# Program order through the output projection, and GpSimd kept to small instructions

## The chip, the cores and the metric

The kernel runs on one core of one Trainium2 chip. The time is device microseconds of one execution; three runs of the kernel before are shown with their median. TensorE (PE) multiplies, VectorE (DVE), ScalarE (ACT) and GpSimd (POOL) work on tiles, and SyncE (SP) issues most transfers. Each engine takes its instructions in the order of its own queue.

## The reference

One pre-norm transformer block: sliding-window attention, and a gated MLP that mixes over the sequence. S = 2048 tokens, D = 640, 32 heads of 20 columns, a window of 256 tokens, two gate halves of Fh = 864 columns.

```python
h  = x + A(layernorm(x))
h2 = h + B(layernorm(h))

def A(x):                                   # wqkv (D, 3D), wo (D, D)
    q, k, v = split_heads(x @ wqkv)         # 32 heads, 20 columns each
    p = softmax(where(window, q @ k.T * 20 ** -0.5, -1e9))
    return merge_heads(p @ v) @ wo

def B(x):                                   # w_in (D, 2 Fh), w_sp (S, S), w_out (Fh, D)
    z = gelu(x @ w_in)
    z1, z2 = z[..., :Fh], layernorm(z[..., Fh:])
    return (z1 * (w_sp @ z2 + b_sp[:, None])) @ w_out
```

## The kernel before

Products that need float32 accuracy are made from two parts: `hi`, the operand rounded for TensorE, and `lo`, the rest. `hi*hi`, `hi*lo` and `lo*hi` are added up in PSUM. So each operand costs a copy (the `hi`, mostly on ACT) and a subtraction (the `lo`, on DVE or POOL).

**Attention.** The scores are computed by steps `s`, one for a group of four heads and one block of 128 keys; step `s` makes the scores of item `s` and the product with V (`pv_item`) of item `s - 2`. The product for 256 tokens is copied out of PSUM into `ot` (L398 on ACT, L400 on DVE) and stored to the scratch `o_d` in DRAM. A 21st column of V gives the sums of the softmax. `inverse_sums` loads them from `o_d`, takes the reciprocal on DVE (L342) and stores it to `r_d`; it is a generator, advanced once per step, for 512 tokens at a time. Another generator, `proj_early`, uses the last sixteen steps to load and split wo (L180, L181) and to load, scale and split the first tiles of the attention's output.

**wo.** The loop at the end of `block_kernel` runs over 16 tiles of 128 tokens. `load_o` brings two tiles of `o_d` (five transfers of 128 KB) and the matching reciprocals; `norm_o` (L146) multiplies them; `split_o` makes `hi` and `lo` (L152 to L155); `proj_o` (L89) does 30 matmuls into one of two accumulators `acc`; L1165 adds x, which gives h. h is stored from ACT's queue (L1166), and `layernorm` (L73 to L79) makes the normed tile `hn`: statistics on DVE, two one-column steps on POOL, the scaling on DVE. `turn_h` transposes it with five PE instructions and stores it to `hn_d`. Into the same loop `win1_prep` weaves the preparation of the first half of w_in (`right_blocks`, L644), and `run(i - NT)` the first operands of the next stage.

**z and the gate.** A list `steps` of PE products follows, and `later` holds what is to be done around each (`at(n, f)`: `f` at step `n`). Eight `z_pair`s make the first half of z. Then come four `z2_pair`s (60 matmuls each, L886; gelu at L890; statistics at L908 to L913; scaling at L918; `right_blocks` makes the seven right operands of a seven-product block multiplication), eight `first_gate`s, four more `z2_pair`s and eight `second_gate`s, with the products of w_sp at L992. During the first second gate the rows of w_out are loaded one by one into a small buffer and split (`put_wout`, L122 and L123). In the z pairs and the gates the matmuls are long and the other engines prepare their operands a few steps ahead.

**Who sets the order.** In a `manual_schedule` context (`ms`) PE, DVE, ACT and SP take their instructions in the order of the program. The context ends at `ms.close()`, just ahead of the wo loop; from there on a planner orders each engine's queue by modelled times. POOL is not in the context's list.

Of the kernel before, what the change touches and what calls it, by code (L numbers as in the profile page):

```python
# [34 lines left out]
def block_kernel(ctx, tc, x, wqk, wv, wo, w_in, wsp, bsp, w_out, out):  # L35
# [13 lines left out]
    o_d = dram.tile([H, 32, S], F32, name="o_d")  # L49
# [31 lines left out]

    def gemm(ps, n, lhs, rhs, ks):

        lh, ll = lhs
        rh, rl = rhs
        for k in range(ks):
            for a, b in ((lh, rh), (lh, rl), (ll, rh)):
                for j in range(2):
                    nc.tensor.matmul(ps[:, j, :n], a(k), b(k, j),  # L89
                                     start=(k == 0 and a is lh and b is rh),  # L90
                                     stop=(k == ks - 1 and a is ll))
# [5 lines left out]
    def open_early(pl):  # L97
        mem["t1"] = pl.tile([P, 2 * KF * D], F32R, name="t1")
        mem["m1"] = pl.tile([P, 6 * D + 4 * P], F32, name="m1")
        mem["xh"] = [pl.tile([P, D], F32, name=f"xh{i}") for i in range(2)]  # L100
        mem["ho"] = [pl.tile([P, D], F32, name=f"ho{i}") for i in range(3)]
# [27 lines left out]
    def load_o(j):  # L129
# [3 lines left out]
        for k in range(KD):  # L133
            nc.sync.dma_start(ot[:, k], o_d[:, 4 * k:4 * k + 4, t])
# [3 lines left out]
        def load_rs():  # L138
            base = r_d[:, t]
            nc.sync.dma_start(rs, bass.AP(tensor=base.tensor, offset=base.offset, ap=[[S, H], [0, 4], [1, 2 * P]]))  # L140
# [3 lines left out]
    def norm_o(i, eng):  # L144
        ot, rs = ots[i]
        eng.tensor_tensor(out=ot, in0=ot, in1=rs[:, None, :].to_broadcast([P, KD, P]), op=OP.mult)  # L146

    def split_o(i, eng):
        ot, _ = ots[i]
        osp = mem["osp2"] if i % 3 == 2 else t1((2 * KD + i % 3 * 2) * D, 2, KD, P)  # L150
        if eng is nc.vector:
            eng.tensor_copy(out=osp[:, 0], in_=ot)  # L152
        else:
            nc.scalar.activation(osp[:, 0], ot, AF.Copy)
        eng.tensor_tensor(out=osp[:, 1], in0=ot, in1=osp[:, 0].bitcast(F32), op=OP.subtract)  # L155
        ots[i] = osp

# [7 lines left out]
    def proj_early():  # L165
# [10 lines left out]
        for _ in range(4):  # L176
            yield
        for k in range(KD):
# [3 lines left out]
            if k in (1, 3):  # L182
                yield
        yield
        rs = load_o(0)
        yield
        yield
        rs()
        yield
        yield  # L190
        load_o(1)()
        yield
        for i in range(2):
            norm_o(i, nc.vector)
            split_o(i, nc.vector)
            yield


    with ExitStack() as ab:
# [132 lines left out]
        def inverse_sums(c):  # L332
            t = tmp3.tile([P, P], F32, tag="inv", bufs=2, name=f"inv{c}")

            def rows(d, step):
                return bass.AP(tensor=d.tensor, offset=d.offset, ap=[[step, H], [P, 4], [1, P]])

            yield
            nc.sync.dma_start(t, rows(o_d[:, DH, c * 512:(c + 1) * 512], 32 * S))
# [3 lines left out]
            nc.sync.dma_start(rows(r_d[:, c * 512:(c + 1) * 512], S), t)  # L343
# [27 lines left out]
        def pv_item(u):  # L371
# [20 lines left out]
            if kb % 2:  # L392
# [4 lines left out]
                if u >= NU - 5 or j == 0 and u < NU - LEAD:  # L397
# [3 lines left out]
                nc.sync.dma_start(o_d[4 * g:4 * g + 4, :, e:e + 256].rearrange("h d t -> (h d) t"), ot)  # L401
            if kb % 4 == 3:
                if g == 7:
                    inverse.append(inverse_sums(c))
# [176 lines left out]
        for s in range(NU + 2):  # L581
# [5 lines left out]
            for hh in range(4):  # L587
# [9 lines left out]
                if hh == 2 + s - NU and s >= NU:  # L597
                    if s == NU:
                        psB.close()
                        psW = pool(psB, "psW", space=PSUM)  # L600
                    pre_ps.append(proj_o(s - NU, psW.tile([P, 2, 512], F32, tag="wo", bufs=3, name=f"wo_ps{s - NU}")))
                if s >= 2:
# [3 lines left out]
                    if hh == 3:  # L606
                        next(pv, None)
            if u1 == NU:
# [12 lines left out]
        for f in inverse:  # L621
            for _ in f:
                pass


    ms.close()
# [78 lines left out]
    def win1_prep(raw):  # L705
        seven, last = win1
        src = w_in[:, :FH].rearrange("k (h c) -> k h c", h=2)
        for k in range(2):
# [5 lines left out]
            for f in right_blocks(lambda: [s[k] for s in seven], *(raw[:, b, h] for b in range(2) for h in range(2)),  # L714
                                  eng=nc.gpsimd):
# [9 lines left out]
    def win2_prep(raw):  # L725
        for k in range(KD):
# [5 lines left out]
            minus(win2[0][:, 1, k], raw, win2[0][:, 0, k].bitcast(F32), nc.gpsimd)  # L732
# [33 lines left out]
    def turn_h(i):  # L766
        ht = mem["ho"][i % 3]
        if i < NT - 2:
# [99 lines left out]
    def z2_pair(q, i, j, k):  # L868
# [6 lines left out]
        def prep(t, first, eng):  # L875
# [3 lines left out]
            else:  # L879
                minus(a[t][:, 1], r3, a[t][:, 0].bitcast(F32), eng)  # L880
# [11 lines left out]
        for t, tile_t in ((0, i), (1, j)):  # L892
# [3 lines left out]
            at(m - (1 if soon else 3), lambda t=t: prep(t, True, None))  # L896
            at(m - (1 if soon else 2), lambda t=t: prep(t, False, nc.gpsimd if t else nc.vector))
# [6 lines left out]
        def stat(t, h):  # L904
# [4 lines left out]
            if h:  # L909
                nc.vector.bn_aggr(out=mv[:, 0:2], in_=st)  # L910
                nc.gpsimd.tensor_scalar(out=mv[:, 2:3], in0=mv[:, 1:2], scalar1=EPS, scalar2=None, op0=OP.add)
                nc.gpsimd.tensor_tensor(out=mv[:, 3:4], in0=mv[:, 2:3], in1=half, op=OP.pow)
                nc.gpsimd.tensor_scalar(out=mv[:, 2:3], in0=mv[:, 0:1], scalar1=mv[:, 3:4], scalar2=-1.0,  # L913
                                        op0=OP.mult, op1=OP.mult)

        def norm(t):
            mv = stats[t][1]
            nc.scalar.activation(z[t], z[t], AF.Identity, bias=mv[:, 2:3], scale=mv[:, 3:4])  # L918
# [11 lines left out]
    def gate_pair(p, c, post, extra):  # L930
# [13 lines left out]
        eng = nc.vector if p else nc.gpsimd  # L944

# [6 lines left out]
        def s13():  # L952
            plus(s1, a21, a22, eng=eng)
            minus(a21, a11, a21, eng)

        def s2():
            minus(a11, s1, a11, eng)
# [263 lines left out]
```

## Time and profile before

| | |
|---|---|
| runs, median of 3 | 1161.44 us (1158.47 to 1166.19) |
| the profiled execution | 1165.89 us |
| its span | 1163.7 us |
| mean granted PE clock | 0.984 |
| busy: PE, DVE, ACT, POOL | 1102.1, 736.8, 553.9, 404.8 us |
| moved by DMA | 165.35 MB |

A row of the timeline is: start, duration, engine, line, operation, output <- inputs, form, count, and in brackets how long the engine had been idle and which instruction or transfer ended that wait. A row of the groups has the busy time and the mean duration in ns, then the idle time before such instructions and what ended it. In the table by stage each engine has its busy time and its count of instructions; PEclk is the granted clock of PE as a share of full speed. Busy times of PE include waiting in its pipeline, so counts of matmuls say more than its busy time.

### The profile page before, as it was taken

What the parts mean: (1) busy time and instruction counts of PE and PEld (TensorE: products, weight loads), DVE (VectorE), ACT (ScalarE), POOL (GpSimd) and SP (SyncE); (2) the same over time, 40 slices, a digit from 0 to 9 for tenths busy, and PEclk for the clock granted to TensorE, in tenths of its full rate; (3) what the DMA queues carried; (4) which work ended last, traced back from release to release, by engine and by line L of the source; (5) the groups of instructions that cost most, each with busy time, mean ns of one, the idle gap of its engine ahead of it and who ended that gap; (6) DMA issues with size and microseconds to landing.
All of it is one profiled execution on the core that took longest, in us unless ns stands there. A gap on an engine that the chain in (4) does not pass through costs nothing.

```text
span 1163.7 us, 28646 instructions
## 1 busy us (share of the span) xinstructions
PE 1102.1 (95%) x11152; PEld 994.7 (85%) x11152; DVE 736.8 (63%) x1961; ACT 553.9 (48%) x1181; POOL 404.8 (35%) x530
## 2 busy tenths in 40 slices
PE   6999999999999999788999998999999799999998
PEld 6998886667877777588999997999999699999998
DVE  5541213788999986679858468655547874655542
ACT  4334433258998889534257566433336531222110
POOL 3124443456666667446421066000117420000000
PEclk9999999999999999889999999999999999999999
DMA  4222355545555543578736512232341454444332
GB/s 149 78 69 80 136 169 201 184 152 176 184 182 176 179 136 125 164 233 270 245 138 210 167 65 73 67 130 87 119 152 39 157 167 152 142 132 143 93 94 68
DMA packets 79800, 165.35 MB, mean 142 GB/s; under 512 B 10752, under 2 KB 43264, under 8 KB 75776
## 3 DMA queue, kind: packets, MB, share of 16 engines
q1 hardware_dynamic: 77360, 158.28, 42.0%
q10 hardware_dynamic: 2304, 5.24, 1.2%
q8 instruction: 87, 1.43, 0.5%
q14 instruction: 49, 0.40, 0.1%
HBM read 108.83 MB, written 54.66 MB: 140 GB/s over the span
## 4 chain that ended last, share of the span: by engine, by line
PE 62%; ACT 8%; issue 7%; POOL 7%; DVE 6%; DMA 6%; SPq 3%; ACTq 0%; POOLq 0%; DVEq 0%
PE g L992 21%; PE out_ps L1057 8%; ACT pt L363 5%; PE pv L386 4%; PE bank L300 3%; PE bank L361 3%; PE zx L835 2%; POOL sg L486 2%; PE zv L835 2%; PE zb L886 2%; PE zy L835 2%; PE zw L835 1%; PE wo_ps L89 1%; PE qk L467 1%; PE qk L468 1%
## 5 line engine op out<-in xcount | busy, mean ns | idle before, releaser
L363 ACT ACTIVATE pt<-bank 128x384 f32<-128x384 f32 (+2 forms) x512 | 202.5, 484 | 29.4 <-PE bank L361 22.3
L992 PE MATMUL g<-zl,aw 128*128 128x432 f32 x768 | 174.4, 363 | 8.8 <-ACT zl L650 8.3
L650 ACT ACTIVATE aw<-fx 128x512 fp32r<-128x512 f32 (+2 forms) x160 | 92.9, 595 | 187.3 <-PE g L992 122.3
L310 DVE CUSTOM_DVE_ANT_0 junk<-bank,strip 128x288 bf16<-128x288 f32 x392 | 156.2, 454 | 15.2 <-PE bank L300 13.8
L992 PEld LDWEIGHTS g<-zl,aw 128*128 128x128 f32 x768 | 145.4, 190 | 17.3 <-ACT zl L650 10.5
L992 PE MATMUL g<-ze,aw 128*128 128x432 f32 x576 | 136.2, 366 | 4.6 <-ACT aw L650 4.5
L386 PE MATMUL pv<-pt,v_sb 128*32 128x192 f32 (+3 forms) x1984 | 130.9, 326 | 10.1 <-DVE ot L400 5.0
L644 DVE TENSOR_TENSOR aw<-fx,aw 128x512 fp32r<-128x512 f32 (+2 forms) x152 | 111.9, 746 | 37.0 <-ACT aw L650 36.3
L992 PEld LDWEIGHTS g<-ze,aw 128*128 128x128 f32 x576 | 109.8, 192 | 10.3 <-ACT aw L650 5.2
L361 PE MATMUL bank<-slot 123*32 123x288 bf16 (+7 forms) x1536 | 110.0, 280 | 2.4 <-issue 1.1
L365 POOL TENSOR_SCALAR_AFFINE_SELECT pt<-pt 128x512 f32<-128x512 f32 x128 | 81.9, 640 | 70.6 <-ACT pt L363 69.3
L1057 PE MATMUL out_ps<-wout,y_sp 128*128 128x320 f32 (+1 forms) x630 | 96.2, 309 | 0.4 <-ACT y_sp L122 0.4
L886 PE MATMUL zb<-win,aw 128*128 128x432 f32 x480 | 95.3, 359 | 0.0
L1057 PEld LDWEIGHTS out_ps<-wout,y_sp 128*128 128x128 f32 (+1 forms) x630 | 94.1, 188 | 1.2 <-ACT y_sp L122 0.7
L886 PEld LDWEIGHTS zb<-win,aw 128*128 128x128 f32 x480 | 89.9, 187 | 4.7
L300 PE MATMUL bank<-slot 120*32 120x288 bf16 (+6 forms) x1280 | 92.2, 277 | 0.9 <-issue 0.8
L483 DVE TENSOR_TENSOR rest<-qk,sg 128x512 f32<-128x512 f32 x40 | 27.7, 692 | 89.5 <-ACT sg L481 89.5
L386 PEld LDWEIGHTS pv<-pt,v_sb 128*32 128x32 f32 x1984 | 61.9, 111 | 17.8 <-issue 14.3
L361 PEld LDWEIGHTS <-slot 123*32 123x32 bf16 x1728 | 60.3, 98 | 17.1 <-issue 8.3
L486 POOL TENSOR_TENSOR sg<-rest,sg 128x512 bf16<-128x512 f32 x40 | 46.5, 1164 | 75.1 <-ACT sg L485 73.2
L368 POOL TENSOR_SCALAR_AFFINE_SELECT pt<-pt 128x512 f32<-128x512 f32 x112 | 71.6, 639 | 0.0
L644 DVE TENSOR_TENSOR row<-g,row 128x432 f32<-128x432 f32 x80 | 48.2, 604 | 36.1 <-PE g L992 32.7
(192 smaller groups left out, 2221.1 us busy)
## 6 DMA issues: line engine op xcount, KB each, us to landing
slot<-qk_d SPq DMA_DIRECT2D x144, 160.0 KB
fx<-wsp_in SPq DMA_DIRECT2D x32, 512.0 KB
qk_d<-sg SPq DMA_DIRECT2D x40, 384.0 KB
fx<-hn_d SPq DMA_DIRECT2D x32, 320.0 KB
o_d<-ot SPq DMA_DIRECT2D x64, 128.0 KB
xb<-qk_d SPq DMA_DIRECT2D x48, 160.0 KB
z_d<-row SPq DMA_DIRECT2D x16, 432.0 KB
g_d<-row SPq DMA_DIRECT2D x16, 432.0 KB
```

What stands on the lines that cost most here:

```text
L300: nc.tensor.matmul(ps[32 * j:32 * j + 32, o:o + w], one(st, 120, 0, hh, q0, 32), k, start=True, stop=True, tile_position=(0, 32 * j))
L310: nc.vector.tensor_tensor_reduce(out=junk[:, :n], in0=ps[:, :n], in1=keep, scale=1.0, scalar=NEG, op0=OP.add, op1=OP.max, accum_out=m_cols ...
L361: nc.tensor.matmul(ps[32 * i:32 * i + 32, b + o:b + o + w], one(st, 123, 1, hh, k0, 32), q, start=True, stop=True, tile_position=(0, 32 * i))
L363: nc.scalar.activation(pt[:, hh, :n], ps[:, :n], AF.Exp, scale=SCALE)
L365: nc.gpsimd.affine_select(out=pt[:, :, :P], in_=pt[:, :, :P], pattern=[[0, 4], [1, P]], base=0, channel_multiplier=-1, compare_op=OP.is_ge ...
L386: nc.tensor.matmul(ps[32 * hh:32 * hh + 32, a - 512 * c:b - 512 * c], v_sb[:, kb, v0:v0 + 32], pt[:, hh, a - kb * P:b - kb * P], start=fir ...
L644: (eng or nc.vector).tensor_tensor(out=out, in0=a, in1=b, op=op)
L650: nc.scalar.activation(out, a, AF.Copy)
L835: nc.tensor.matmul(ps, a[x], b[:, y], start=start and m + x + y == 0, stop=stop and m == n - 1 and x == 1, skip_group_check=True)
L886: nc.tensor.matmul(b[0][:, :HF], a[t][:, x, kk], win2[0][:, y, kk, h * HF:(h + 1) * HF], start=kk + x + y == 0, stop=kk == KD - 1 and x == 1)
L992: nc.tensor.matmul(ps, w[m][:, x, k], zc[k][m][:, y], start=start and k + x + y == 0, stop=stop and k == 3 and x == 1, skip_group_check=True)
L1057: nc.tensor.matmul(ps[j][:, :HD], src[:w, a, k, :], e1["wout"][:w, b, k, j * HD:(j + 1) * HD], start=(k == 0 and a + b == 0), stop=(k == K ...
```

## The change

- `ms.close()` moves from ahead of the wo loop to the third step of the z stage: the wo loop runs in program order. The loop is written anew: an iteration `i` does the projection of tile `i`, the addition and statistics of tile `i - 1`, scaling and split of the attention's output of tile `i + 2`, the scaling of `hn` of `i - 1` and the transposes of `i - 2`.
- The scratch `o_d` is laid out by column, head and token, wo's rows are ordered to match, and `load_o` is one transfer instead of five.
- `inverse_sums` works on 256, 256, 512, 512 and 512 tokens, with one more step between the load and the reciprocal. `proj_early` starts one step sooner and takes one row block of wo per step.
- Within a step the PV product comes ahead of the early `proj_o`; two of the last `ot` copies move from ACT to DVE.
- Every wide subtraction or addition that POOL did from wo on is done by DVE. POOL keeps the one-column steps of the statistics, of which there are now three per tile in wo.
- The final scaling of `hn` moves from DVE to ACT (`scaled`), and the stores of h move from ACT's queue to SP's.
- In a `z2_pair` the scaling of the first row and the operands that follow from it come one step later in program order.

```diff
-    o_d = dram.tile([H, 32, S], F32, name="o_d")
+    o_d = dram.tile([32, H, S], F32, name="o_d")
...
+    def stats_of(mv, st):
+        nc.vector.bn_aggr(out=mv[:, 0:2], in_=st)
+        nc.gpsimd.tensor_scalar(out=mv[:, 2:3], in0=mv[:, 1:2], scalar1=EPS, scalar2=None, op0=OP.add)
+        nc.gpsimd.tensor_tensor(out=mv[:, 3:4], in0=mv[:, 2:3], in1=half, op=OP.pow)
+        nc.gpsimd.tensor_scalar(out=mv[:, 2:3], in0=mv[:, 0:1], scalar1=mv[:, 3:4], scalar2=-1.0,
+                                op0=OP.mult, op1=OP.mult)
+
+    def scaled(dst, src, mv):
+        nc.scalar.activation(dst, src, AF.Identity, bias=mv[:, 2:3], scale=mv[:, 3:4])
...
-        for k in range(KD):
-            nc.sync.dma_start(ot[:, k], o_d[:, 4 * k:4 * k + 4, t])
+        base = o_d[:, :, t]
+        nc.sync.dma_start(ot, bass.AP(tensor=base.tensor, offset=base.offset, ap=[[S, P], [P * S, KD], [1, 2 * P]]))
...
-        eng.tensor_tensor(out=osp[:, 1], in0=ot, in1=osp[:, 0].bitcast(F32), op=OP.subtract)
         ots[i] = osp
+        return lambda: nc.vector.tensor_tensor(out=osp[:, 1], in0=ot, in1=osp[:, 0].bitcast(F32), op=OP.subtract)
...
-        for _ in range(4):
+        for _ in range(3):
             yield
         for k in range(KD):
...
-            if k in (1, 3):
-                yield
-        yield
-        rs = load_o(0)
+            if k == 2:
+                rs0 = load_o(0)
+            yield
+        rs0()
+        rs1 = load_o(1)
         yield
         yield
-        rs()
-        yield
-        yield
-        load_o(1)()
+        rs1()
         yield
         for i in range(2):
-            norm_o(i, nc.vector)
-            split_o(i, nc.vector)
+            norm_o(i)
+            split_o(i, True)()
             yield
+        yield
+        norm_o(2)
...
-                if u >= NU - 5 or j == 0 and u < NU - LEAD:
+                if u >= NU - 2 or j == 0 and u < NU - LEAD:
...
-            if kb % 4 == 3:
-                if g == 7:
-                    inverse.append(inverse_sums(c))
+            if g == 7 and (kb % 4 == 3 or kb == 1):
+                n = 256 if kb < 4 else 512
+                inverse.append(inverse_sums((kb + 1) * P - n, n))
...
-        for f in inverse:
-            for _ in f:
-                pass
-    ms.close()
...
-            minus(win2[0][:, 1, k], raw, win2[0][:, 0, k].bitcast(F32), nc.gpsimd)
+            minus(win2[0][:, 1, k], raw, win2[0][:, 0, k].bitcast(F32))
...
-        f = right_blocks(lambda: zc[k], *blocks, nc.vector if k == 3 else nc.gpsimd)
+        f = right_blocks(lambda: zc[k], *blocks)
         at(n0 + 1, lambda: stat(0, 0))
-        at(n0 + 2, lambda: (stat(0, 1), norm(0), f[0](), f[1](), f[2]()))
-        at(n0 + 3, lambda: stat(1, 0))
+        at(n0 + 2, lambda: stat(0, 1))
+        at(n0 + 3, lambda: (stat(1, 0), norm(0), f[0](), f[1](), f[2]()))
...
-        eng = nc.vector if p else nc.gpsimd
...
-                split(e1["wout"][:, 0, k], e1["wout"][:, 1, k], e1["h"][k // 4], nc.gpsimd)
+                split(e1["wout"][:, 0, k], e1["wout"][:, 1, k], e1["h"][k // 4])
...
-    for i in range(NT):
-        if 1 < i + 1 < NT:
-            split_o(i + 1, nc.gpsimd)
-        if i % 2 == 0 and i + 4 < NT:
-            load_o(i // 2 + 2)()
+    stat_h = {}
+
+    def add_h(i):
+        h3 = hs[i].rearrange("p (a b) -> p a b", a=2)
+        nc.vector.tensor_tensor(out=h3, in0=pre_ps.pop(0)[:, :, :HD], in1=h3, op=OP.add)
+        nc.sync.dma_start(h_d[i], hs[i])
+
+    def bn_h(i):
+        st, mv = stat_h[i] = stat_tiles(f"c{i}")
+        for j in range(2):
+            nc.vector.bn_stats(out=st[:, j, :], in_=hs[i][:, j * HD:(j + 1) * HD])
+        stats_of(mv, st)
+
+    lows = {}
+    for i in range(1, NT + 1):
+        if i < NT:
+            for f in inverse:
+                next(f, None)
+                if i == 2:
+                    next(f, None)
+        if i == 1:
+            split_o(2)()
+        if 1 < i < NT:
+            pre_ps.append(proj_o(i, acc_tile(f"wo_ps{i}")))
+        if i > 1:
+            add_h(i - 1)
         if i + 2 < NT:
-            norm_o(i + 2, nc.vector)
-        for n in (2, 3, 4) if i == 0 else (i + 4,) if i + 4 < NT else ():
+            norm_o(i + 2)
+            lo = split_o(i + 2)
+        if i == 1:
+            add_h(0)
+        if i < NT:
+            run(i - NT)
+        bn_h(i - 1)
+        if i + 2 < NT:
+            lo()
+        if i == 1:
+            load_o(2)()
+        if i % 2 and i < NT - 5:
+            load_o(i // 2 + 3)()
+        for n in (2, 3, 4) if i == 1 else (i + 3,) if i + 3 < NT else ():
             load_x2(n)
-        run(i - NT)
-        ps = pre_ps[i] if i < 2 else proj_o(i, acc_tile(f"wo_ps{i}"))
+        next(w1, None)
+        scaled(hn(i - 1), hs.pop(i - 1), stat_h.pop(i - 1)[1])
         if i > 1:
             turn_h(i - 2)
-        nc.vector.tensor_tensor(out=h3, in0=ps[:, :, :HD], in1=h3, op=OP.add)
-        nc.scalar.dma_start(h_d[i], xt)
-        layernorm(hn(i), xt, D, f"c{i}")
-        next(w1, None)
-        if i % 2:
+        if i % 3 == 1:
             next(w1, None)
...
     for n in range(len(steps)):
         run(n)
-        if n < 2:
-            turn_h(NT - 2 + n)
         if n == 2:
+            turn_h(NT - 1)
+            ms.close()
+        if n == 3:
             open_d()
```

More of the change, by code (lines that the diff above doesn't have):

```diff
@@ L100, in open_early @@
         mem["xh"] = [pl.tile([P, D], F32, name=f"xh{i}") for i in range(2)]
+        mem["inv"] = [pl.tile([P, P], F32, name=f"inv{i}") for i in range(2)]
         mem["ho"] = [pl.tile([P, D], F32, name=f"ho{i}") for i in range(3)]
@@ L330, in block_kernel, with inverse_sums @@
         p_tiles, pv_tiles, inverse = {}, {}, []
-        def inverse_sums(c):
-            t = tmp3.tile([P, P], F32, tag="inv", bufs=2, name=f"inv{c}")
+        def inverse_sums(t0, n):
+            t = mem["inv"][len(inverse) % 2][:, :n // 4]
             def rows(d, step):
-                return bass.AP(tensor=d.tensor, offset=d.offset, ap=[[step, H], [P, 4], [1, P]])
+                return bass.AP(tensor=d.tensor, offset=d.offset, ap=[[step, H], [n // 4, 4], [1, n // 4]])
             yield
-            nc.sync.dma_start(t, rows(o_d[:, DH, c * 512:(c + 1) * 512], 32 * S))
+            nc.sync.dma_start(t, rows(o_d[DH, :, t0:t0 + n], S))
+            yield
             yield
@@ L342, in inverse_sums @@
             nc.vector.reciprocal(out=t, in_=t)
-            nc.sync.dma_start(rows(r_d[:, c * 512:(c + 1) * 512], S), t)
+            nc.sync.dma_start(rows(r_d[:, t0:t0 + n], S), t)
             yield
@@ L607, in block_kernel @@
                         next(pv, None)
+                if hh == 2 + s - NU and s >= NU:
+                    if s == NU:
+                        psB.close()
+                        psW = pool(psB, "psW", space=PSUM)
+                    pre_ps.append(proj_o(s - NU, psW.tile([P, 2, 512], F32, tag="wo", bufs=3, name=f"wo_ps{s - NU}")))
             if u1 == NU:
```

57 lines of the change are left out of this document (23 added, 34 removed).

## The prediction

> **What bounds the kernel now.** I read the page's head first, then the table by stage, then the timeline of the matmul engine (PE) in the stages that the change touches.
>
> ```profile
> span 1163.7 us, 28646 instructions
> ```
>
> ```profile
> core 0: us, PE busy (x) PEld busy (x) DVE busy (x) ACT busy (x) POOL busy (x), PEclk, DMA share, GB/s
> 466.00:486.00 20.00, 13.42 (x260) 9.26 (x256) 8.77 (x14) 12.78 (x36) 11.37 (x17) 0.83 0.57 181
> 486.00:582.40 96.40, 85.99 (x565) 83.42 (x566) 81.93 (x135) 30.70 (x54) 49.25 (x52) 0.93 0.72 236
> 716.00:741.00 25.00, 20.14 (x85) 17.54 (x83) 19.57 (x35) 14.60 (x28) 6.95 (x10) 0.86 0.10 35
> 741.00:903.00 162.00, 162.00 (x826) 154.81 (x827) 89.86 (x135) 68.67 (x122) 32.42 (x35) 1.00 0.33 108
> 903.00:947.00 44.00, 35.42 (x166) 32.35 (x165) 37.67 (x57) 21.61 (x39) 21.34 (x16) 0.92 0.47 159
> ```
>
> PE is the bound: from 741 to 903 it never rests. What a change here can win is what PE loses elsewhere, and the table names four places: the attention's tail (466 to 486), wo (486 to 582), the start of the first gate products (716 to 741), and the start of the second ones (903 to 947). In each the clock column is below 1 too, so an idle PE also pays afterwards. What PE does there at its own pace, and where it stops:
>
> ```profile
> 471.19 1.08 PE L386 MATMUL pv<-pt,v_sb 128*32 128x256 f32 x8 [5.00 <-DVE ot L400]
> ...
> 487.69 5.93 PE L89 MATMUL wo_ps<-t 128*128 128x320 f32 x30 [2.22 <-DVE t L152]
> ...
> 512.27 7.16 PE L89 MATMUL wo_ps<-t 128*128 128x320 f32 x30 [1.55 <-DVE xh L1165]
> ...
> 538.23 5.88 PE L89 MATMUL wo_ps<-t,osp 128*128 128x320 f32 x28 [2.92 <-DVE mvc L74]
> ...
> 567.61 4.64 PE L89 MATMUL wo_ps<-t 128*128 128x320 f32 x30
> ...
> 572.55 4.65 PE L89 MATMUL wo_ps<-t,osp 128*128 128x320 f32 x30
> ```
>
> ```profile
> 740.94 115.34 PE g L992 x588
> ```
>
> Undisturbed, a wo tile with its five transposes takes 572.55 - 567.61 = 4.94 us, so 16 tiles take 79.0. They took 582.4 - 487.69 = 94.7: **15.7 us lost in wo**, always behind DVE, in gaps of 1.5 to 3 us and in slow matmuls after them (7.16 and 5.93 for 30). A gate matmul takes 115.34 / 588 = 0.196 us. 85 of them are 16.7 of the 25 us from 716: **8.3 lost**. 166 are 32.5 of the 44 from 903: **11.5 lost**. In the tail 6.6 of 20 us are idle and the clock of 0.83 costs up to 3.4: **10 lost**. All four: 45 us, the most that the change can bring.
>
> **Part 1: the attention's tail.** DVE holds the PV products up here, since PE can't go on before the copy `ot` at L400.
>
> ```profile
> 463.65 0.93 DVE L180 CAST t<-m 128x640 fp32r<-128x640 f32 x1 [1.99 <-DMA m<-wo_in]
> ...
> 470.63 0.42 DVE L400 COPY ot<-pv 128x256 f32<-128x256 f32 x1
> ...
> 485.06 0.95 DVE L342 RECIPROCAL inv<-inv 128x128 f32<-128x128 f32 x1 [6.07 <-DMA inv<-o_d]
> 485.93 0.76 DVE L146 TENSOR_TENSOR m<-m 128x640 f32<-128x640 f32 x1
> ```
>
> ```profile
> 464.79 6.82 DMA o_d<-ot
> ...
> 477.99 2.44 DMA o_d<-ot
> ```
>
> The change spreads wo's five splits one per step instead of two, starts the reciprocals with the first 256 tokens and gives each load one more step. But the first split still waits for wo, whose load isn't issued sooner, and it now stands one step earlier ahead of `ot`. Two more `ot` copies come to DVE from ACT (2 x 0.42). On SP the load of the sums now stands ahead of the next store of `o_d` and waits for the one before it to land (6.82 us in the crowd, 2.44 without), and the reciprocal on DVE waits behind that. So the 5.00 splits into smaller stalls rather than going; the 6.07 wait before the first `norm_o` goes, and with it most of the 2.22 on PE. I take **2 us gained**, with bounds of 8 (both waits and their clock) and -4 (a wait of 6.82 instead of 2.44 in front of `ot`).
>
> **Part 2: wo in program order.** In an iteration DVE now adds h (i-1), scales o (i+2), takes statistics (i-1), and makes the low part (i+2), which POOL did; ACT takes over the final scaling of h. PE needs its operands two tiles, some 10 us, later, and has two accumulators.
>
> ```profile
> L146 DVE TENSOR_TENSOR m<-m 128x640 f32<-128x640 f32 x16 | 15.4, 995 | 6.6 <-DMA m<-o_d 3.5 <-DMA hn_d<-ho 1.7 <-DMA r_d<-inv 1.4
> L73 DVE BATCH_NORM_STATS2 stc<-xh 128x6 f32<-128x320 f32 x30 | 13.1, 478 | 0.2
> L1165 DVE TENSOR_TENSOR xh<-wo_ps,xh 128x640 f32<-128x640 f32 x16 | 12.9, 808 | 0.8 <-PE wo_ps L89 0.8
> L79 DVE TENSOR_SCALAR m<-xh,mvc 128x640 f32<-128x640 f32 x15 | 12.4, 824 | 5.3 <-POOL mvc L76 5.3
> L644 DVE TENSOR_TENSOR zl<-wraw,zl 128x432 fp32r<-128x432 f32 x10 | 7.9, 812 | 0.0
> L74 DVE BATCH_NORM_AGGREGATE mvc<-stc 128x2 f32<-128x12 f32 x15 | 3.0, 202 | 0.2
> L155 POOL TENSOR_TENSOR t<-m,t 128x640 fp32r<-128x640 f32 x9 | 15.1, 1680 | 10.5 <-ACT t L154 9.1 <-PE pv L386 1.4
> ```
>
> ```profile
> 687.84 2.88 DVE L644 TENSOR_TENSOR ze<-row,ze 128x432 fp32r<-128x432 f32 x2 [0.47 <-ACT ze L650]
> ...
> 733.41 1.12 DVE L644 TENSOR_TENSOR zl<-row,zl 128x432 fp32r<-128x432 f32 x2
> ```
>
> What does an instruction cost DVE once POOL is quiet? The same 432-wide pair took 2.88 us with a POOL instruction running and 1.12 with POOL idle; the 640-wide scaling took 0.76 alone against a mean of 0.995. So DVE per tile: 2 x 0.76 + 0.808 + 2 x 0.478 + 0.202 = 3.49, times 14 is 48.8. The prepared w_in blocks: 24 low parts and differences x 0.56 = 13.4. Two reciprocals 1.9, the first z pair's operands about 4 (an estimate: ten narrow ones of some 0.4). Sum **68 us in PE's 79**. With before's means (0.995 twice, 0.812): 3.96 x 14 + 19.5 + 5.9 = 81, 2 too many. So DVE fits, by 11 or by -2; the 432-wide pair settles it for the first, since POOL is left with three one-column instructions per tile. The added work on ACT, 15 scalings near 0.82 in place of L79's, is 12 us on an engine that is busy 30.7 of 96.4.
>
> Queues: the 16 stores of h move from ACT's queue to SP's and each waits there for DVE's addition; behind it stand the loads of o, x and w_in. At the first iteration SP also has the last load of sums, which waits for the last store of `o_d` (2.44) and holds up tiles 4 to 7 and x: that is covered by wo tiles 1 to 3 (3 x 4.94). One load of 640 KB takes the place of five of 128 KB over the same bytes. The DMA share of 0.72 becomes 0.72 x 96.4 / 82 = 0.85: full, but with loads three tiles ahead. I leave 3 us of loss (the slow start 5.93 - 4.64 = 1.3, and something at the change of pools at the end): **13 us gained**. Bounds: all 15.7, or 2, if DVE needs its 81 and waits on top as L146 and L79 do now (81 + 6.6 + 5.3 = 93 of 94.7).
>
> **Part 3: the first gate products.** Here POOL's small statistics stand behind its own large instructions.
>
> ```profile
> 719.66 0.20 DVE L910 BATCH_NORM_AGGREGATE mvz<-stz 128x2 f32<-128x12 f32 x1
> ...
> 721.32 1.51 POOL L644 TENSOR_TENSOR zl<-row,zl 128x432 fp32r<-128x432 f32 x1
> 722.79 0.56 POOL L912 TENSOR_TENSOR mvz<-mvz,half 128x1 f32<-128x1 f32 x1
> 723.46 0.26 POOL L913 TENSOR_SCALAR mvz<-mvz 128x1 f32<-128x1 f32 x1
> ...
> 723.76 1.11 ACT L918 ACTIVATE row<-row,mvz 128x864 f32<-128x864 f32 x1 [2.96 <-POOL mvz L913]
> ...
> 725.51 0.47 PE L992 MATMUL g<-zl,aw 128*128 128x432 f32 x1 [4.40 <-ACT zl L650]
> ```
>
> From the aggregate (719.86) to L913's end (723.72) are 3.9 us; without the large instructions it is three small ones, about 0.3 + 0.56 + 0.26 with gaps of 0.1, or 1.3. So the scaling starts 2.5 us sooner and PE's 4.40 shrinks to 1.9; late next is the second row's statistics, 1.6 behind. "One step later" puts the scaling behind the other row's statistics; it is a change of order on ACT where the wait of 2.96 stands, at nothing by this row, at most one product step (15 x 0.196 = 2.9) against it. DVE's three extra instructions in this stretch (3 x 0.56) are paid by what POOL no longer takes from it. With half a us of clock I take **3 us gained** of 8.3, bounds 6 and 0.
>
> The clock: after the 2.92 us gap 28 matmuls took 5.88 us where 30 take 4.64. [...]
>
> **Part 4: the second gate products.** The same chain again (2.5), and a second stop:
>
> ```profile
> 922.60 4.37 POOL L123 TENSOR_TENSOR wout<-hr,wout 128x640 fp32r<-128x640 f32 x1 [3.87 <-ACT wout L122]
> ...
> 929.94 0.74 ACT L122 ACTIVATE wout<-hr 128x640 fp32r<-128x640 f32 x1 [3.39 <-DMA hr<-w_out_in]
> ...
> 931.25 3.21 PE L992 MATMUL g<-ze,aw 128*128 128x432 f32 x8 [4.49 <-ACT aw L650]
> ```
>
> ACT waits for the next w_out rows, whose buffer came free only after POOL's 4.37. On DVE the same takes 0.76, up to 3.6 sooner, but in a queue that is busy 37.67 of 44 us, and a DVE that waits for such a row now holds the gate operands behind it. I take 2.5. Sum **5 us gained** of 11.5, bounds 9 and -4.
>
> **Sum.** 2 + 13 + 3 + 5 = 23 us. The profiled execution took 1165.89 (span 1163.7 and 2.2 around it), so 1142.9 by its own time. The runs' median is 1161.44, 4.5 lower; 23 us off that is **1138 us**. Bounds: 8 + 15.7 + 6 + 9 = 39 off gives 1122; -4 + 2 + 0 - 4 gives 1167.
>
> **The rivals.** *Only program order works (0.16).* From the fourth step on the order comes from a planner's modelled times, as before; if it puts other DVE work ahead of the statistics, parts 3 and 4 bring nothing: 15 off, 1146. For it: DVE is 19.57 of 25 and 37.67 of 44 busy there. Against it: the 1.51 on POOL does go.
>
> *Operands come late (0.13).* At a DMA share of 0.85 the loads of o or x miss their tile; DVE stands in order at `norm_o`, and h, statistics and low parts behind it. For it: L146 waited 6.6 us for transfers already. Against: loads go out three tiles ahead. Then parts 1 and 2 bring 2 and the rest 8: 1151.
>
> *DVE becomes the bound (0.09).* If its instructions stay as long as now without POOL, a z2 pair costs it 11 x 0.736 + 2 x 0.995 + 4 x 0.589 + 0.4 = 12.9 us against PE's 60 x 0.196 = 11.8.
>
> ```profile
> L908 DVE BATCH_NORM_STATS2 stz<-row 128x6 f32<-128x432 f32 x16 | 9.4, 589 | 0.6 <-ACT row L890 0.6
> L644 DVE TENSOR_TENSOR zl<-row,zl 128x432 fp32r<-128x432 f32 x13 | 9.2, 736 | 4.9 <-ACT zl L650 4.9
> ```
>
> Four pairs bring DVE 4.4 us late to each gate start, 8.8 in all; w_out adds 7 x 0.76 = 5.3 at the full stretch from 903; wo gains only its lower bound of 2. That is 12 slower: 1173. It decides from 0.64 us per 432-wide instruction on ((11.8 - 4.76) / 11). Against it: 0.56 with POOL idle. [...]
>
> **Chances.** Forecast 0.62, the others as given. About 1% (11.6 us) can be told from no change. Forecast and first rival lie beyond it, less 0.01 for their edge: faster 0.77. Late operands fall within 1%, with that edge: 0.14. Slower 0.09. Leaving out a tenth on each side, 1122 to 1163; the forecast's own range is 1128 to 1148.
>
> **What would show it.** Right: no POOL instruction over 1 us after 490; wo's 16 tiles within 83 us and DVE idle at times there; the 432-wide DVE instruction near 0.56; L913 within 1.5 us of its aggregate; the gap at the gate starts under 2.5 us. Wrong: DVE full through wo with PE waiting for it, `norm_o` waiting for transfers, or the gate gaps as long as before behind DVE.

## The result: no gain

The changed kernel took 1166.59 us (median of 12 runs, 1163.33 to 1169.96) against 1160.81 for the kernel before in the same session: a ratio of 1.0046, 95% interval 1.0026 to 1.0065. That is a small loss, inside the 1% called "same" in the prediction, and 28.6 us above the forecast of 1138. The parts cancelled: some gained, and others lost, more than this. Times and ratios, here and below, are of fast runs; one run of e1, 1789.71 us at a granted clock of 0.558, was slow and is left out.

The profile after, from the page's head:

```profile
span 1164.1 us, 28590 instructions
...
PE 1098.0 (94%) x11152; PEld 992.7 (85%) x11152; DVE 728.5 (63%) x2022; ACT 567.7 (49%) x1194; POOL 304.8 (26%) x472
```

Where TensorE (PE) begins each stage, from the view of one tile's instructions (the two times near the end of a line are the first and last start), after and then before. `zv` is the first product of the z stage, `zb` the product of the `z2_pair`s:

```profile
L99 PE MATMUL wo_ps<-t x330: 302/309/636, 500.7 to 591.9; 128*128 128x320 f32 x165
...
L844 PE MATMUL zv<-zl,aw x120: 352/358/444, 593.8 to 683.2; 128*128 128x432 f32 x120
...
L895 PE MATMUL zb<-win,aw x480: 353/359/462, 679.9 to 914.2; 128*128 128x432 f32 x160
```

```profile
L89 PE MATMUL wo_ps<-t x330: 302/309/607, 487.7 to 581.8; 128*128 128x320 f32 x165
...
L835 PE MATMUL zv<-zl,aw x120: 352/357/447, 582.4 to 666.9; 128*128 128x432 f32 x120
...
L886 PE MATMUL zb<-win,aw x480: 354/359/363, 664.8 to 903.3; 128*128 128x432 f32 x160
```

Cutting both spans there gives a ledger. Wo's first product comes 13.0 us later (500.7 - 487.7). From it to the first zv product: 93.1 against 94.7, 1.6 gained. From zv to zb: 86.1 against 82.4, 3.7 lost. From zb to the end: 484.2 against 498.9, 14.7 gained, 10.5 of it after the last zb product. In all 0.4 lost.

The gate starts are as wished. They come later in the changed kernel: its first gate product starts at 730.80 instead of 715.67, and its last zb product ends at 914.6 instead of 903.6. So the two stretches are moved by 15.13 and 11 us, to have the same work in them. The table by stage of the changed kernel, columns as in the prediction:

```profile
500.70:593.80 93.10, 83.33 (x576) 81.83 (x572) 66.27 (x125) 40.57 (x65) 24.72 (x45) 0.93 0.73 250
731.13:756.13 25.00, 23.13 (x116) 21.15 (x115) 20.11 (x36) 14.75 (x27) 2.12 (x4) 1.00 0.18 60
914.00:958.00 44.00, 42.76 (x233) 40.23 (x232) 38.19 (x69) 20.29 (x36) 3.46 (x6) 1.00 0.58 184
```

At the first gate start, 116 matmuls instead of 85 in the 25 us and a clock of 1.00; at the second, 233 instead of 166 in the 44 us. The first row is wo: DVE is busy 66.27 of 93.1 us, so wo isn't slow for want of DVE. PE's own timeline there:

```profile
499.92 0.87 PE L398 MATMUL pv<-pt,v_sb 128*32 128x192 f32 x8 [7.18 <-DVE ot L412]
500.72 5.93 PE L99 MATMUL wo_ps<-t 128*128 128x320 f32 x30
...
516.43 4.64 PE L99 MATMUL wo_ps<-t 128*128 128x320 f32 x30
530.22 1.33 PE L784 MATMUL ht_ps<-ident,m 128*128 128x128 f32 x5 [9.15 <-ACT m L90]
...
572.17 4.65 PE L99 MATMUL wo_ps<-t 128*128 128x320 f32 x30
576.65 0.71 PE L784 MATMUL ht_ps<-ident,m 128*128 128x128 f32 x5
577.12 4.64 PE L99 MATMUL wo_ps<-t 128*128 128x320 f32 x30
```

Two stops, 7.18 ahead of wo and 9.15 inside it, and then tiles every 4.95 us (577.12 - 572.17), as forecast. Where the second comes from, on SP and on ScalarE (ACT):

```profile
500.86 7.28 SPq L414 DMA_DIRECT2D o_d<-ot  x2
508.24 0.54 SPq L355 DMA_DIRECT2D r_d<-inv  x1
511.05 0.58 SPq L350 DMA_DIRECT2D inv<-o_d  x1
...
512.78 0.43 SPq L145 DMA_DIRECT2D m<-o_d  x1
...
515.42 2.76 SPq L138 DMA_DIRECT2D xh<-x_in  x3
518.22 1.19 SPq L721 DMA_DIRECT2D wraw<-w_in_in  x2
```

```profile
528.79 0.56 ACT L660 ACTIVATE zl<-wraw 128x432 fp32r<-128x432 f32 x1 [6.11 <-DMA wraw<-w_in_in]
529.26 0.91 ACT L90 ACTIVATE m<-xh,mvc 128x640 f32<-128x640 f32 x1
```

The scaling of a tile (L90) stands on ACT behind the first w_in tile, whose load SP issues only after the last store of `o_d`, the sums that wait for it, two loads of o and three of x. And before wo, attention itself has waits that it hadn't. `m_d` is a small scratch in DRAM: attention stores the maxima of its rows there and loads them back into `slot` and `xb`, operands of the scores. The waits between 250 and 470 us (in total, times, longest), after:

```profile
PE bank L373 <- DMA slot<-m_d: 6.9, 4, 3.7
PE bank L373 <- DMA xb<-m_d: 4.4, 1, 4.4
```

```profile
SPq L338 <- DMA m_d<-m: 37.6, 15, 4.4
```

and before:

```profile
PE bank L361 <- DMA slot<-m_d: 0.7, 1, 0.7
```

```profile
SPq L327 <- DMA m_d<-m: 19.5, 14, 3.4
```

The stores and loads of `m_d` weren't touched by the change. They share SP's queue with the stores of `o_d`, whose layout was.

### The profile page after: what moved, and what is told of

Its sections match the earlier page's. It is cut to its first block, busy times and chain, and to the rows that moved or that the text cites. A ratio compares the mean times of both kernels' runs of the same rounds, so it can differ in the third digit from the quotient of the medians.

```text
span 1164.1 us, 28590 instructions
## 1 busy us (share of the span) xinstructions
PE 1098.0 (94%) x11152; PEld 992.7 (85%) x11152; DVE 728.5 (63%) x2022; ACT 567.7 (49%) x1194; POOL 304.8 (26%) x472
## 4 chain that ended last, share of the span: by engine, by line
PE 43%; DVE 5%; DMA 5%; ACT 2%; issue 2%; POOL 1%; SPq 1%; POOLq 0%; ACTq 0%; DVEq 0%
PE g L994 20%; PE out_ps L1059 8%; PE zb L895 5%; PE zx L844 2%; PE zv L844 2%; PE zy L844 2%; PE zw L844 1%; PE yt_ps L1048 1%; DVE zl L654 1%; DMA wraw<-w_in_in 1%; PE wo_ps L99 1%; DMA fx<-hn_d 1%; DMA m<-o_d 1%; DMA xh<-x_in 1%; DVE row L654 1%
## 5 line engine op out<-in xcount | busy, mean ns | idle before, releaser
L660 ACT ACTIVATE aw<-fx 128x512 fp32r<-128x512 f32 (+3 forms) x160 | 93.2, 595 | 164.0 <-PE g L994 114.2
L994 PE MATMUL g<-zl,aw 128*128 128x432 f32 x768 | 171.4, 358 | 0.7 <-ACT zl L660 0.4
L398 PE MATMUL pv<-pt,v_sb 128*32 128x192 f32 (+3 forms) x1984 | 133.8, 329 | 17.2 <-DVE ot L412 11.0
L994 PE MATMUL g<-ze,aw 128*128 128x432 f32 x576 | 133.7, 360 | 2.8 <-ACT aw L660 1.7
L654 DVE TENSOR_TENSOR aw<-fx,aw 128x512 fp32r<-128x512 f32 (+3 forms) x160 | 102.3, 646 | 39.9 <-ACT aw L660 34.2
L994 PEld LDWEIGHTS g<-ze,aw 128*128 128x128 f32 x576 | 106.8, 188 | 8.5 <-ACT aw L660 2.4
L373 PE MATMUL bank<-slot 123*32 123x288 bf16 (+8 forms) x1536 | 110.2, 279 | 1.4 <-ACT pt L375 1.1
L377 POOL TENSOR_SCALAR_AFFINE_SELECT pt<-pt 128x512 f32<-128x512 f32 x128 | 82.5, 645 | 78.0 <-ACT pt L375 76.3
L311 PE MATMUL bank<-slot 120*32 120x288 bf16 (+5 forms) x1280 | 94.4, 281 | 0.1
L84 POOL TENSOR_SCALAR mvz<-mvz 128x1 f32<-128x1 f32 x16 | 5.1, 318 | 295.1 <-DVE mvz L83 289.6
L380 POOL TENSOR_SCALAR_AFFINE_SELECT pt<-pt 128x512 f32<-128x512 f32 x112 | 73.9, 660 | 0.0
```

Of the source, the lines that this page charges most:

```text
L311: nc.tensor.matmul(ps[32 * j:32 * j + 32, o:o + w], one(st, 120, 0, hh, q0, 32), k, start=True, stop=True, tile_position=(0, 32 * j))
L373: nc.tensor.matmul(ps[32 * i:32 * i + 32, b + o:b + o + w], one(st, 123, 1, hh, k0, 32), q, start=True, stop=True, tile_position=(0, 32 * i))
L377: nc.gpsimd.affine_select(out=pt[:, :, :P], in_=pt[:, :, :P], pattern=[[0, 4], [1, P]], base=0, channel_multiplier=-1, compare_op=OP.is_ge ...
L398: nc.tensor.matmul(ps[32 * hh:32 * hh + 32, a - 512 * c:b - 512 * c], v_sb[:, kb, v0:v0 + 32], pt[:, hh, a - kb * P:b - kb * P], start=fir ...
L654: (eng or nc.vector).tensor_tensor(out=out, in0=a, in1=b, op=op)
L660: nc.scalar.activation(out, a, AF.Copy)
```

## The experiments

All times are medians, with the ratio to the kernel before and its 95% interval.

| kernel | us | ratio |
|---|---|---|
| changed | 1166.59 | 1.0046 (1.0026 to 1.0065) |
| e1: changed, old layout of o_d | 1155.25 | 0.9926 (0.9895 to 0.9957) |
| e2: before, new layout | 1183.52 | 1.0190 (1.0154 to 1.0226) |
| e3: changed, GpSimd's wide work back | 1183.84 | 1.0190 (1.0142 to 1.0238) |
| e4: changed, each store as four | 1217.33 | 1.0484 (1.0451 to 1.0518) |
| e5: e1, wo's loads ahead of the sums | 1148.09 | 0.9885 (0.9861 to 0.9910) |
| e6: e5, last pv copies on ACT | 1143.71 | 0.9854 (0.9830 to 0.9877) |
| e7: before, padded heads | 1178.64 | 1.0148 (1.0122 to 1.0173) |
| e8: e6, z's start reordered | 1138.20 | 0.9800 (0.9778 to 0.9822) |
| e9: e8, load_o(2) first | 1136.42 | 0.9782 (0.9756 to 0.9808) |
| e10: e9, first row at its old step | 1134.50 | 0.9774 (0.9745 to 0.9804) |
| e11: before, GpSimd part alone | 1150.73 | 0.9898 (0.9865 to 0.9930) |
| e12: e9, load_o(2) earlier still | 1138.89 | 0.9799 (0.9774 to 0.9824) |

### The layout: e1, e2, e7, e4

```diff
 # e1, in the changed kernel (load_o, load_rs, the sums and wo's row order follow)
-    o_d = dram.tile([32, H, S], F32, name="o_d")
+    o_d = dram.tile([H, 32, S], F32, name="o_d")
-                nc.sync.dma_start(... ap=[[S, 4], [H * S, 32], [1, 256]]), ot)
+                nc.sync.dma_start(o_d[4 * g:4 * g + 4, :, e:e + 256].rearrange("h d t -> (h d) t"), ot)
```

> The changed kernel with o_d laid out as before, [H, 32, S]: one store is again 128 rows in a row, load_o is five transfers, the load of reciprocals goes by heads first. All else of the change stays. Theory A (the new layout makes every store of o_d slow, and the transfers queued with it): attention's last load from m_d comes back from 467.2 us to about 460, the gaps of 4.45 and 3.67 behind xb and slot are gone, the first wo_ps product comes from 500.7 to about 490, and the time falls by 11 to 16 us, to 1150 to 1155. Theory B (the layout is innocent; the 7.5 us of attention and the 6.2 us of its tail come from the new order of sums, loads and products): no change there, time 1165 to 1169, or up by what five transfers cost SP.

> The kernel before with the new layout of o_d alone, with the store, load_o, the loads of sums and of reciprocals and the order of wo's rows that belong to it; nothing else of the change. Theory A: attention's last load from m_d moves from 460.4 us to 466 to 468, the sums and reciprocals land later at its end, time up by 7 to 14 us, to 1168 to 1175. Theory B: within 3 us of 1161, or below it by what four fewer load issues per two tiles save.

Undone in the changed kernel, the layout gives 0.012 of ratio back, some 14 us; done alone in the kernel before, it costs 1.9%, 22 us. Theory A in both in kind; in e2 the price is above the 7 to 14 us that it named. In e1 PE has no wait for `m_d` in this view and SP's is back at

```profile
SPq L338 <- DMA m_d<-m: 18.5, 14, 3.3
```

But e1 and e2 change loads and addresses too. e7 changes how the store's 128 rows are grouped, and beside that only moves each head's rows on by one row for every head before it:

```diff
 # e7, in the kernel before
-    o_d = dram.tile([H, 32, S], F32, name="o_d")
+    o_d = dram.tile([H, 33, S], F32, name="o_d")
-                nc.sync.dma_start(o_d[4 * g:4 * g + 4, :, e:e + 256].rearrange("h d t -> (h d) t"), ot)
+                nc.sync.dma_start(... ap=[[33 * S, 4], [S, 32], [1, 256]]), ot)
```

> The kernel before with one row of padding behind each head of o_d (33 rows a head instead of 32), so that a store's 128 rows of 1 KB no longer follow each other at one stride: its pattern has four groups of 32 rows, at four heads, in the order of the old layout. Nothing else. Theory A (a store whose outermost dimension has four entries is carried by four of the sixteen DMA engines): its packets take four times as long as before, one store some 1.8 us instead of 0.45, and the time rises nearly as far as with the new layout alone, by 12 to 22 us. Theory C (the new layout is slow because neighbouring rows of a store lie far apart in memory, or because of the loads that changed with it): within 4 us of before.

1.5% slower, 17 us, with the waits of the new layout, in the same view:

```profile
PE bank L361 <- DMA slot<-m_d: 9.4, 4, 3.3
PE bank L361 <- DMA xb<-m_d: 4.8, 2, 3.1
```

```profile
SPq L327 <- DMA m_d<-m: 38.7, 14, 4.6
```

So most of the layout's price is the form of the store, not where its rows lie. The 0.4% between e7 and e2 stays open: their intervals overlap, and in e2 the load of the reciprocals begins with four groups too, which wasn't tried alone. What the form changes is in the packet counts of the page, before and then e7:

```profile
DMA packets 79800, 165.35 MB, mean 142 GB/s; under 512 B 10752, under 2 KB 43264, under 8 KB 75776
```

```profile
DMA packets 79032, 165.35 MB, mean 140 GB/s; under 512 B 9984, under 2 KB 42496, under 8 KB 75008
```

The bytes are the same; 768 small packets are gone, all of 4 bytes in the trace: 12 for each of the 64 stores. Single stores, where their packets met few others, show the same: before, the 128 packets of 1 KB were over in 0.51 to 0.57 us in five stores and in 1.04 to 1.36 in three, mostly with 16 small ones behind them; in three stores of the changed kernel and three of e7 they took 1.76 to 1.80, mostly with 4. Over the first five the DMA share, the mean busy share of the core's 16 DMA engines, was 0.71 to 0.76, so 11 to 12 engines' worth; over the three of the changed kernel 0.25 to 0.28, or 4 to 4.5. That fits four engines for a store in four groups, but no run names the engines that carried it. SP is also held longer by an issue, here two stores in the middle of attention, before and after:

```profile
388.26 0.34 SPq L401 DMA_DIRECT2D o_d<-ot  x1
```

```profile
387.11 0.55 SPq L414 DMA_DIRECT2D o_d<-ot  x1
```

e4 tried to keep the layout and spread the store:

```diff
+                for a in range(4):
+                    nc.sync.dma_start(o_d[:, 4 * g + a, e:e + 256], ot[32 * a:32 * a + 32])
```

> The changed kernel with the new layout kept, but every store of o_d given as four transfers, one for each head (32 rows of 1 KB each), and the load of reciprocals as four, one for each quarter of the partitions. Theory A, in the form that a store is slow because its outermost dimension has four entries: each of the four now has 32, the stores land as fast as before, attention gets back most of its 7.5 us, less what three more issues per store take on SP (some 0.4 to 0.55 us each, 1.2 to 1.7 us a store, 128 stores in all, most of it beside TensorE's work): time 1155 to 1165. If SP's issues bound it instead: above 1167. Theory B (layout innocent): above 1167 as well, by the issues alone, with the packets of a store as slow as before.

4.8% slower. Four issues took SP 1.80 us instead of 0.55, 64 times (the expectation said 128 stores; there are 64), and PE waited 24.8 us for `slot` and 17.6 for `xb` from `m_d`. The transfers themselves were as fast as Theory A has it: a quarter's 32 packets were over in 0.30 us, with 16 small packets behind them. So I read the loss as SP's issues binding attention, which the expectation allowed for.

### Wo's start and attention's tail: e5, e6, e8, e9, e12

```diff
 # e5, in e1
     for i in range(1, NT + 1):
+        if i == 1:
+            for n in (2, 3, 4):
+                load_x2(n)
+            next(w1, None)
+            load_o(2)()
         if i < NT:
             for f in inverse:
```

> e1 (the change with o_d's old layout) with another order on SP where wo's loop begins: the loads of x for tiles 2 to 4, the first loads of w_in and load_o(2) are issued ahead of the steps of the sums of attention, not behind them and behind load_o(3). In e1 the first w_in tile is issued at 509.9 us, ScalarE waits 7.33 for it with the scaling of a finished tile behind it, and TensorE stands 7.56 at 517.67. Theory A (the order of SP's queue makes that gap): w_in is issued at about 499, the gap falls below 2.5, tiles 4 to 15 follow each other at 4.95, first zv 5 to 6.5 us earlier counted from the first wo_ps product, time 1148 to 1152. Theory B (TensorE waits there for the operands of tile 4, which load_o and the sums set, whatever comes first): the gap keeps 5 us or more, only its releaser changes, time within 2 us of e1.

In e1 PE waited 7.56 us at 517.67 for L90 on ACT; in e5

```profile
509.31 1.33 PE L782 MATMUL ht_ps<-ident,m 128*128 128x128 f32 x5 [4.58 <-ACT m L90]
```

From the first wo product to the first zv it took 89.5 us, e1 92.2; the ratio fell by 0.0041, 5 us, with intervals that overlap, and the time of 1148.09 is in the range of Theory A. The gap didn't fall below 2.5 as A said: w_in was out at 494.8, but ACT now waited 7.42 for `m<-o_d`, tile 4's operand, B's cause. Both were there, one behind the other.

```diff
 # e6, in e5
-                if u >= NU - 2 or j == 0 and u < NU - LEAD:
+                if u >= NU - 5 or j == 0 and u < NU - LEAD:
```

> e5 with attention's last copies of pv back on ScalarE (u >= NU - 5, as before), where the change gave all but the last to VectorE. In e1 TensorE stands 4.26 us at 489.16 and 2.96 at 478.91 behind copies on VectorE, which stand in program order behind norm_o, the splits of tiles 0 and 1 and two reciprocals, while ScalarE is idle for 11.4 us. Theory A (these copies are late because of what stands ahead of them on VectorE): both gaps fall below 1.5, the first wo_ps product 3 to 5 us earlier, time 2 to 5 us below e5. Theory B (the operands of tile 0 come at the same time, so that TensorE only waits one product later): the gap appears ahead of the first wo_ps product instead, time within 1.5 us of e5.

The gap of 4.26 is gone (0.61 there now); the smaller one, 2.46 in e5, is 2.34. Time 4.4 us below e5, with intervals that overlap; the first wo product 3.5 earlier. Theory A for the copies that moved, by the gap more than by the time.

```diff
 # e8, in e6
+        if i == NT:
+            turn_h(i - 2)
         scaled(hn(i - 1), hs.pop(i - 1), stat_h.pop(i - 1)[1])
-        if i > 1:
+        if 1 < i < NT:
             turn_h(i - 2)
```

> e6 with the transposes of the last but one tile ahead of the scaling of the last one in program order, where the z stage begins. In e1 TensorE stands 2.59 us at 586.24 for the copy of these transposes, which on ScalarE stands behind the scaling of tile 15 and so behind GpSimd's steps for it; the second pool of banks opens only then. Theory A: the gap falls below 0.7, first zb 1.5 to 2.6 us earlier counted from the first zv product, time 1 to 3 us below e6. Theory B (the next z products wait for the operands of tile 14 or 15 in any case): the gap moves and the time is that of e6 within 1 us.

From zv to zb 82.1 us instead of 86.4, before's 82.4 again; the gap of 2.58 is gone. That is more than the gap, since slow matmuls followed it (in e6 nine took 3.23 us, undisturbed 1.92). Time 5.5 below e6, above what A expected.

> e8 with load_o(2) ahead of the loads of x and w_in where wo's loop begins, instead of behind them. In e8 the attention's output for tile 4 is issued from 496.0 to 499.9 us; VectorE waits 7.73 for it with the statistics of tile 1 queued behind, and TensorE stands 4.46 at 509.67 for the scaling that needs them. Theory A (that load sets the gap): it is issued 2.4 us earlier, the gap falls to 1 to 2.5, time 1 to 3.5 us below e8. Theory B (w_in and x, now behind it, are late instead): gap as long, with another releaser, time within 1 us of e8.

> e9 with the attention's output for tiles 4 and 5 issued earlier still, at the end of attention's tail ahead of its last two stores of o_d, its reciprocals where they are in e9. Theory A: the wait of VectorE ahead of tile 4 and TensorE's gap behind it are gone (below 0.6), time 1 to 3 us below e9. Theory B (the last stores, and the sums that read them, come 3 us later and hold up more): time equal to e9 or above it.

In e8 the gap is

```profile
509.67 0.77 PE L782 MATMUL ht_ps<-ident,m 128*128 128x128 f32 x5 [4.46 <-ACT m L90]
```

and in e9, with load_o(2) moved ahead of the x loads in e5's block,

```profile
501.73 0.77 PE L782 MATMUL ht_ps<-ident,m 128*128 128x128 f32 x5 [1.21 <-ACT m L90]
503.24 4.66 PE L99 MATMUL wo_ps<-t 128*128 128x320 f32 x30 [0.74 <-DVE xh L1154]
```

So that load set the gap. From wo's first product to zv it still took 86.7 us (e8: 87.1), since small waits for statistics came in behind; the times of e8, e9 and e12 can't be told apart. Theory B for e12, as far as it can be seen.

### GpSimd and the later step: e3, e11, e10

e3 hands GpSimd its wide instructions from the z stage on back, in the changed kernel; e11 takes them from it in the kernel before and changes nothing else:

```diff
-minus(win2[0][:, 1, k], raw, win2[0][:, 0, k].bitcast(F32), nc.gpsimd)
+minus(win2[0][:, 1, k], raw, win2[0][:, 0, k].bitcast(F32))
...
-        f = right_blocks(lambda: zc[k], *blocks, nc.vector if k == 3 else nc.gpsimd)
+        f = right_blocks(lambda: zc[k], *blocks, nc.vector)
...
-        eng = nc.vector if p else nc.gpsimd
+        eng = nc.vector
... (the low halves of the hn tiles and of wout likewise)
```

> The changed kernel with GpSimd doing again the wide work that it did before from the z stage on: the low half of win2, the low halves of every second hn tile, the sums of the Strassen blocks but the last, the first gate product's sums, the low half of wout. Wo's loop, the layout and the order of the second rows stay as changed. Theory A (the two gate starts gained 4.3 and 12.7 us by this part): both gains go, the gaps at the starts of the gates come back to over 4 us, time up by 12 to 17 us, to 1178 to 1184. Theory B (the gates gained by the later step of z's first row, or only because wo came late): time within 4 us of 1166.6.

> The kernel before with the wide GpSimd work from the z stage on moved to VectorE (low halves of win2, of hn tiles and of wout, the sums of the Strassen blocks, the first gate product's sums) and nothing else of the change: old layout, old wo loop with its planner, z's first row at its old step. Theory A (this part alone makes the gain at the gate starts, 17 us between the changed kernel and the one with GpSimd's work back): 12 to 17 us below before, 1145 to 1150. Theory B (it needs the later step, or VectorE becomes the bound without it): less than 6 us below before.

e3: 17 us above the changed kernel, Theory A. Its gaps at the gate starts are back, at 4.39 and 3.37 ("over 4" was expected):

```profile
745.07 1.73 PE L996 MATMUL g<-zl,aw 128*128 128x432 f32 x3 [4.39 <-ACT zl L660]
```

```profile
930.70 4.51 PE L996 MATMUL g<-zl,aw 128*128 128x432 f32 x9 [3.37 <-ACT zl L660]
```

e11: 11 us below before (interval 8 to 16), just short of A's range and far from B's, and from zb to the end 484.5 us, the changed kernel 484.2. This part alone makes the gain.

```diff
 # e10, in e9
-        at(n0 + 2, lambda: stat(0, 1))
-        at(n0 + 3, lambda: (stat(1, 0), norm(0), f[0](), f[1](), f[2]()))
+        at(n0 + 2, lambda: (stat(0, 1), norm(0), f[0](), f[1](), f[2]()))
+        at(n0 + 3, lambda: stat(1, 0))
```

> e9 with z's first row scaled at its old step, right behind its second half's statistics, in all z2 pairs; GpSimd keeps its small steps only. Theory A (the later step is worth something of its own, because ScalarE otherwise stands on GpSimd's three steps with the next pair's work behind it): TensorE's waits in the second half of z and at the starts of the gates grow, time 2 to 6 us above e9. Theory B (with no wide work on GpSimd these steps are short, and the step is worth nothing): within 1.5 us of e9.

482.2 us from zb to the end, e9 482.5; the times can't be told apart. Theory B: no worth of the later step can be seen.

## Why the prediction was wrong

**The step that failed: the layout of `o_d`.** The prediction looked only at its load, "One load of 640 KB takes the place of five of 128 KB over the same bytes", and priced the 64 stores, which the same line turns from one group of 128 rows into four of 32, at nothing. The whole layout cost some 14 us in the changed kernel and 22 in the one before, the form of the stores alone 17 (e7). None of the rivals has it: "Operands come late" looks at wo's loads. It is the part that turned a gain into no gain, and it lies in a stage, attention ahead of its tail, that the prediction left out. But it is only about half of the 28.6 us that the forecast missed by: e1, without it, was still no faster than 0.9926. The next step that failed is in Part 2.

**Part 1**, 2 us gained with bounds of 8 and -4: wo began 13.0 later, outside them. Without the layout what is left, 2.3 in e1, is inside, and within what profiles of one code differ by. The mechanism was named ("Two more `ot` copies come to DVE from ACT", the reciprocal waiting behind the sums), but priced by the copies' own 2 x 0.42, not by what stands ahead of them on an in-order DVE. There the first `norm_o` waited 6.59, and the copies that stand behind it came at 495.77 and 499.41:

```profile
493.20 0.94 DVE L157 TENSOR_TENSOR m<-m 128x640 f32<-128x640 f32 x1 [6.59 <-DMA inv<-o_d]
494.17 0.82 DVE L163 CAST t<-m 128x640 fp32r<-128x640 f32 x1
```

The row names the load of the sums; in the chain of the work that ended last, the load of the reciprocals stands ahead of this `norm_o`:

```profile
487.52 5.58 DMA m<-r_d
```

In e1 the same `norm_o` waited 3.38, so part of the wait came with the layout. Giving the copies back to ACT was worth 4.4 by the medians of e5 and e6.

**Part 2**, 13 us with bounds of 15.7 and 2: 1.6 came, and 3.7 went again at z's start. DVE's load was right (68 forecast, 66.27 measured) and so was the tile at 4.94. What failed is the sentence that SP's wait for the last sums "is covered by wo tiles 1 to 3 (3 x 4.94)". It counted that wait (2.44) and not the 10 us from the end of the last store's row on SP (500.86 + 7.28 = 508.14) to w_in's issue (518.22), nor that ACT, in order, holds a finished tile behind w_in (its statistics ended at 524.68, L90 began at 529.26). With the order mended and the old layout, e9 takes 86.7, 8.0 gained: the mechanism holds, the size was nearer 8 than 13. "Something at the change of pools at the end" was a wait of 2.60 and its slow matmuls (nine took 3.39 us, undisturbed 1.92), 4 us in all, and one line of order (e8).

**Parts 3 and 4**, 3 and 5 us: 4.2 and 10.5 by the ledger. Right in kind, and the second above its bound of 9. The longest gap at a gate start was 1.27. What was too small is the clock, for which I counted half a us: it was 1.00 in both stretches, in place of 0.86 and 0.92. DVE's instructions took 0.60 for 432 columns in the mean, with GpSimd busy for 2.12 of the 25 us and 3.46 of the 44: near the 0.56 of the forecast and under the 0.64 from which "DVE becomes the bound" begins, which fell with them. Two signs failed without harm. From the end of the aggregate to the end of the third small GpSimd step it took 1.4 to 2.6 us for the four rows next to the gate starts, where 1.3 was forecast and 1.5 was the limit. And five of these steps after 490 took 1.03 to 1.31, where none was to take over 1 us.

The repairs of e9 bring the time to 1136.42, next to the forecast of 1138; but by other terms than the forecast's, 8 more from zb on and 5 fewer from wo, and with a layout that the change doesn't have. Whether the new layout would cost its 14 us on top of e9 wasn't tried.

## What to carry over

A layout is priced on the side that writes it too: count the groups of every transfer that the new shape touches, however far its stage is from the one you mean to speed up. Where program order takes the place of a planner, walk each in-order queue through the first iteration, and put a load whose consumer has something finished behind it ahead of anything that waits for a landing. And a kernel whose time didn't move may hold a large gain: e9, the same idea with the old layout and a few lines in another order, is 2.2% faster than the kernel before (0.9782, 0.9756 to 0.9808).

## What I had not expected of the hardware

- 64 stores of 128 KB, unchanged in bytes and in rows of 1 KB, cost 17 us when their outermost dimension was 4 (e7): SP's wait for the stores of `m_d`, 24 KB each, rose from 19.5 to 38.7 us.
- Up to wo the kernel before and e11 are the same code, yet their profiles start wo at 487.7 and 482.6 us; e1 and e5 at 490.0 and 484.7. A term of 2 or 3 us ahead of that point can't be read from two profiles; it takes the medians.
- Matmuls ran slowly after waits much shorter than the 9.15 (30 took 6.04 us after that one, 4.64 undisturbed), and not at once. In e6, after a wait of 2.58, six took 1.45 us, but the nine behind them 3.23, where nine take 1.92 undisturbed; the granted clock was 1.00 from 571.6 to 573 and 0.57 from 573 to 577. In e5, after a wait as long, the six took 1.87 already:

```profile
578.21 1.87 PE L842 MATMUL zx<-zl,aw 128*128 128x432 f32 x6 [2.58 <-ACT ho L658]
```
